# Reordering VectorE's work in the fused mLSTM and gated feed-forward kernel: weighing, decay differences and state additions in chunks 1 to 4

## The chip, the cores and the metric

The kernel runs on one core of a Trainium2 chip. The metric is the device time of one execution in microseconds (us); lower is better. The engines are called PE (TensorE's matrix products; PEld is its weight loads), DVE (VectorE), ACT (ScalarE), POOL (GpSimd) and SP (SyncE, which issues most DMAs). "L459" is line 459 of the kernel.

## The reference

Two blocks follow each other: an mLSTM cell over 4 batches, 8 heads, 768 steps and head width 40, and a feed-forward block on its output as 3072 tokens of width 320.

```python
for t in range(S):
    m_new = np.maximum(f_gate[:, :, t] + m, i_gate[:, :, t])
    f_stab = np.exp(f_gate[:, :, t] + m - m_new)
    i_stab = np.exp(i_gate[:, :, t] - m_new)
    m = m_new
    C = f_stab[..., None, None] * C + i_stab[..., None, None] * np.einsum('bhd,bhe->bhde', vt, kt)
    n = f_stab[..., None] * n + i_stab[..., None] * kt
    h_tilde = np.einsum('bhde,bhe->bhd', C, qt)
    nq = np.einsum('bhd,bhd->bh', n, qt)[:, :, None]
    y[:, :, t] = sigmoid(o_gate[:, :, t]) * h_tilde / np.maximum(np.abs(nq), 1.0)
x = y as (B * S, H * D)
h = x @ w_in            # 320 -> 2048
g = h * np.cos(h)
out = g @ w_out         # 2048 -> 320
```

## The kernel before

**Tiling.** The 768 steps are cut into 6 chunks of 128. A *cell* is one chunk of one batch with all 8 heads; cell n is chunk n // 4 of batch n % 4, so there are 24. Within a cell the recurrence is done in its chunkwise form: a 128 x 128 table of decays per head weighs the scores of queries and keys, and a state per batch (`st`, 40 x 41 per head) carries what earlier chunks left.

**The main loop.** `both_parts(c, b)` is a pair of *slots*. In each slot the feed-forward block does the up-projection of 256 hidden features for the 512 tokens of chunk c (class `Up`) and, later in the slot, a part of a down-projection (`down`, `down_first`, by a written plan). Beside that work, the pair computes one cell of the next chunk, n = 4 (c + 1) + b. So chunk c = 1 handles cells 8 to 11, chunk 2 cells 12 to 15, chunk 3 cells 16 to 19 and chunk 4 cells 20 to 23; chunk 5 has no cell. The first slot of a pair is called the even slot here, the second the odd slot. Chunk 0 has weights to prepare as well and an order of its own; from cell 7 on (`TURNED`) a cell works with its result transposed.

**Up.** An up-projection fills two PSUM tiles `pup`, halves e = 0 and 1, from a pool of two buffers: the next slot's `pup` of a half can only begin when this slot's gates have read it. Per half: ACT rounds (`near`, L639), DVE takes the remainder (`rest`, L642), ACT takes the sine (`sin`, L647, which gives a cosine of h by the quarter turn added before), and DVE multiplies (`gate`, L659, two instructions a half; L654 in chunk 0).

**The cell in the even slot.**
- `scores(n)` on PE writes two PSUM tiles `ps` (L453). They come from the pool `ps_a`, which has two buffers and also serves `hp` and `pu` below.
- `weigh(n)` on DVE multiplies them into the decays `E` (L459, two instructions).
- `decay_exponents(n + 1)` is the first step of the next cell's decays: a difference on DVE (L375, 128 x 1024), and a mask on POOL (L376). `decay(n + 1)` is the exponential on ACT (L384).
- `values_turned(n)` on PE writes two tiles `hp` from the state (L490) and from the weighed scores (L496).
- `normalize_turned(n)` on DVE (L510 to L522) reads `hp` and writes the next chunk's input, partly by a detour through DRAM; `fade(n)` multiplies the state by its decay (L577, two instructions, DVE).

In some even slots a down-projection ends and DVE also adds its parts together (`put_together`, seven L765) ahead of L510.

**The cell in the odd slot.** `seam(n)` on PE computes the state's increment `pu` (L596). `state(n)` on DVE adds it to `st` (L612, two instructions). `turn_blocks(n + 1)` and `turn_gates(n + 1)` (L414 to L425) prepare the next cell.

**POOL** does the mask, the sums `sg` of gated tiles for the down-projection (`sums`, L723), the weighing of keys (`kw`, L397), and in chunk 1 differences `T` of the output weights (L696).

**Order.** The whole program is under `tc.manual_schedule()`: each engine executes its instructions in the order in which this Python code emits them, and waits on semaphores for its inputs and for buffers that come free.

Of the kernel before, what the change touches and what calls it, by code (L numbers as in the profile page):

```python
# [29 lines left out]
def kernel(  # L30
# [39 lines left out]
    TURNED = 2 * B - 1  # L70
# [238 lines left out]
    def sigmoid(c, bs=slice(0, B)):  # L309
        o = sig[c][:, bs.start * DM:bs.stop * DM]  # L310
        nc.scalar.activation(out=o, in_=o, func=AF.Sigmoid)
# [53 lines left out]
    def psum_o():  # L365
        return ps_o.tile([128, HP, C], FP, name="pm", tag="o")

    def cols(n, j, width):
        c, b = divmod(n, B)
        return tab[:, c, j, ts(b, H)].unsqueeze(2).to_broadcast([128, H, width])  # L370


    def decay_exponents(n):
        E = Es[n]
        nc.vector.tensor_tensor(out=E, in0=E, in1=cols(n, 0, C), op=OP.subtract)  # L375
        nc.gpsimd.affine_select(out=E, in_=E, compare_op=OP.is_ge, fill=1.0e30, base=0,  # L376
                                pattern=[[0, H], [1, C]], channel_multiplier=-1)
# [5 lines left out]
    def decay(n):  # L383
        nc.scalar.activation(out=Es[n], in_=Es[n], func=AF.Exp, scale=-1.0)  # L384
# [61 lines left out]
    def scores(n):  # L446
        pool, tag = psum(n)
        qT, kT = qkT[n]
        ps = [pool.tile([128, HP, C], FP, name="ps", tag=tag) for _ in range(2)]
        for p in range(HP):  # L450
            for j in range(2):
                r = slice(64 * j, 64 * j + (64 if n < TURNED else D))
                nc.tensor.matmul(ps[j][:, p], kT[r, p], qT[r, p], start=True, stop=True)  # L453
        pss[n] = ps

    def weigh(n):
        for j in range(2):
            w = Es[n].rearrange("p (a j) t -> p a j t", j=2)[:, :, j]
            nc.vector.tensor_tensor(out=w, in0=pss[n][j], in1=w, op=OP.mult)  # L459

    def values_kept(n):

        pool, tag = (ps_o, "o") if n == B else psum(n)
        heads_of[n] = None
        if n >= B:
            pq = pool.tile([128, H, D1], FP, name="pq", tag=tag)
            for p in range(HP):
                nc.tensor.matmul(pq[:, 2 * p:2 * p + 2].rearrange("p j d -> p (j d)"), qkT[n][0][:, p],
                                 st[n % B][:, p].rearrange("p j d -> p (j d)"), start=True, stop=True)
            heads_of[n] = pq  # L470
# [94 lines left out]
    def halves(n):  # L565
        for j in range(2):
            r = slice(64 * j, 64 * j + D)
            yield j, r, st[n % B][r, :, j]
# [37 lines left out]
    def state(n):  # L606
        if n < N - B:
            for j, r, s in halves(n):
                if n < B:
                    nc.scalar.copy(out=s, in_=pus[n][r])  # L610
                else:
                    nc.vector.tensor_tensor(out=s, in0=s, in1=pus[n][r], op=OP.add)  # L612
# [101 lines left out]
    def sums(T):  # L714

        for c, s, p, in_parts in plan.get(T, ()):
            if in_parts:
                S = p2.tile([128, 4, C], FP, name="sg", tag="wt")
                A11, A21, A12, A22 = (gs[c, p, s][:, ts(i, C)] for i in range(4))
                engine = nc.vector if T > 8 * NC + 1 else nc.gpsimd  # L720
                for i, (x, y, op) in enumerate(((A21, A22, OP.add), (S[:, 0], A11, OP.subtract),
                                                (A11, A21, OP.subtract), (A12, S[:, 1], OP.subtract))):
                    engine.tensor_tensor(out=S[:, i], in0=x, in1=y, op=op)  # L723
                sg[c, s, p] = S
# [109 lines left out]
    def warm(k, bank=None):  # L834

        for _ in range(k):
            nc.tensor.matmul(bank or pw, nil, nil.unsqueeze(1).to_broadcast([128, HP, 128]), start=True, stop=True)
# [129 lines left out]
    def out_parts():  # L967
        p, piece = outs.pop(0)
        return p, parts(*piece)

    def out_join(p, h, last=None):
        join(*h, last)
        if p + 3 < NF // 2:
            outs.append((p + 3, weights_out(p + 3)))

    def both_parts(c, b):

        n = (c + 1) * B + b
        cell = n < N
        begin = c == b == 0
        more = cell and n + 1 < N
        f2 = 2 * b
        slot = NF // 2 * c + f2
        sums(slot)
        up = Up(c, f2, cell_after_first if begin else None)
        if cell:
            scores(n)  # L990
            if begin:
                values_kept(n)

                warm(6, psum_o())
        for e in range(2):
            up.near(e)
        if begin:
            weigh(n)
        for e in range(2):
            up.rest(e)  # L1000
        if cell and not begin:
            weigh(n)
        if begin or more and c > 0:
            decay_exponents(n + 1)
        for e in range(2):
            up.sin(e)
            up.gate(e)
        if n == TURNED:
            turn_gates(n)
        if c == 0 and b == 1:  # L1010
            sigmoid(1, slice(1, B))
        if begin:
            sigmoid(1, slice(0, 1))
        h = ()
        if c == 0 and not begin:
            out_join(*out_parts())
        if pieces:
            h = parts(*pieces.pop(0))
        rests = []
        ends = any(step[2] == NP - 1 for step in plan.get(slot, ()))  # L1020
        if ends:
            rests = down(slot)
        if begin or more and c > 0:
            decay(n + 1)
        elif more:
            decay_by_bias(n + 1)
        if 0 < slot <= NP:
            down_first(slot - 1)
        elif slot and not ends:
            down(slot)  # L1030
        for rest in rests:
            rest()
        if cell:
            if n < TURNED:
                load(n + 2)
                if not begin:
                    values_kept(n)
                values(n)
                normalize(n)
                if h:  # L1040
                    join(*h)
            else:
                values_turned(n)
                if h:
                    join(*h)

                normalize_turned(n)
                if n + 2 < N:
                    load(n + 2, "q")
                last_in(n)  # L1050
                if n + 2 < N:
                    load(n + 2, "bkv")
            if TURNED <= n + 2 < N:
                load_G(n + 2)
            if n + 3 < N:
                load_E(n + 3)
            if b == B - 2 and c + 2 < NC:
                load_o(c + 2)
            fade(n)
            if n + 1 == TURNED:  # L1060
                turn_blocks(n + 1)
        h = ()
        sin_next()
        if pieces:
            h = parts(*pieces.pop(0))
        sums(slot + 1)
        up = Up(c, f2 + 1)
        if cell:
            seam(n)
        for e in range(2):  # L1070
            up.near(e)
        for e in range(2):
            up.rest(e)
        if cell and n < TURNED:
            seam_out(n)
        if cell:
            state(n)
        if h:
            join(*h)
        for e in range(2):  # L1080
            up.sin(e)
            up.gate(e)
        if b == B - 1 and 0 < c < NC - 2:
            sigmoid(c + 2)
            sin_next()
        if more:
            weigh_k(n + 1)
        if c == 1 and b < B - 1:
            two_differences(2 * b + 2)
        if pieces:  # L1090
            join(*parts(*pieces.pop(0)))
        if c == 0:
            down_first(f2)
        else:
            for rest in down(slot + 1):
                rest()
        if pieces:
            join(*parts(*pieces.pop(0)))
        if c == 0:
            if b + 2 < B:  # L1100
                pieces.extend(weights_in(b + 2))
            h = out_parts()
        if more and n + 1 < TURNED:
            turn(n + 1)
            turn_out(n + 1, c > 0)
        elif more and n + 1 > TURNED:
            turn_blocks(n + 1)
        if c == 0:
            out_join(*h)
            if b == B - 1:  # L1110
                more_units()
                two_differences(0)
                sigmoid(2)
                sin_next()
        if more and n + 1 > TURNED:
            turn_gates(n + 1)
# [43 lines left out]
```

## Time and profile before

| | before |
|---|---|
| time, median of 3 runs | 533.53 us (532.84 to 539.57) |
| the profiled execution's own time | 533.63 us |
| span of its profile | 531.9 us |
| granted PE clock | 0.998 |
| PE busy | 519.4 us, 98% |
| PE weight loads | 343.2 us, 65% |
| DVE busy | 395.9 us, 74% |
| ACT busy | 264.7 us, 50% |
| POOL busy | 210.0 us, 39% |

The span runs from the first to the last instruction of the program; the execution's own time is 1.7 us longer. Busy times of engines overlap. Matrix products are pipelined and their ends are modelled, so a wait of PE can lie within its busy time. In lines of the timeline the first number is the start in us from the beginning of the span, the second the length; then engine, line, operation, written tile <- read tiles, shapes and the count of merged instructions. A bracket at the end gives idle time ahead of it and what ended it. PE does pairs of chunk 1 from 127.6 to 205.3, of chunk 2 to 281.9, of chunk 3 to 361.7 and of chunk 4 to 440.5.

### The profile page before, as it was taken

The numbers are of one execution on the slowest core, as the hardware profiler recorded it, in microseconds if no ns is written. First come the engines' busy times: TensorE is split into PE (matmuls) and PEld (weight loads), VectorE is DVE, ScalarE is ACT, GpSimd is POOL, SyncE is SP. The second block draws the span as 40 slices with busy tenths as digits, with TensorE's granted clock in tenths as the row PEclk, the third lists the DMA queues.
The fourth block names the chain that finished last, engine by engine and source line by source line (L and its number), as shares of the span: only waits on it lengthen the run. The fifth ranks groups of instructions, "written<-read, shape, count | busy, mean of one in ns | idle before, by whom it ended". The sixth has DMA issues, their size and how long they took to land.

```text
span 531.9 us, 10613 instructions
## 1 busy us (share of the span) xinstructions
PE 519.4 (98%) x3855; PEld 343.2 (65%) x3855; DVE 395.9 (74%) x864; ACT 264.7 (50%) x418; POOL 210.0 (39%) x409
## 2 busy tenths in 40 slices
PE   8989999999999999999999999999999999999996
PEld 6956565555565656556656577577577576657596
DVE  6797858889888987977978978978878864325253
ACT  4799696676633546453457354357354232313210
POOL 7523333434925631131522533533434425344350
PEclk9999999999999999999999999999999999999999
DMA  9999999813465376266276256356354100000000
GB/s 133 229 232 237 219 219 228 197 33 84 126 129 106 74 148 141 77 133 137 58 146 145 76 110 129 87 138 138 85 105 86 41 11 25 6 0 26 0 26 25
DMA packets 134860, 57.80 MB, mean 109 GB/s; under 512 B 70248, under 2 KB 130872, under 8 KB 134808
## 3 DMA queue, kind: packets, MB, share of 16 engines
q1 hardware_dynamic: 134664, 56.93, 48.5%
q8 instruction: 30, 0.49, 0.4%
q14 instruction: 22, 0.18, 0.1%
q0 software_dynamic: 96, 0.18, 0.1%
q10 hardware_dynamic: 48, 0.02, 0.0%
HBM read 50.76 MB, written 6.34 MB: 107 GB/s over the span
## 4 chain that ended last, share of the span: by engine, by line
PE 71%; DVE 13%; DMA 5%; issue 3%; SPq 3%; ACT 3%; POOL 1%; DVEq 0%; POOLq 0%; ACTq 0%
PE po L727 27%; PE pup L631 26%; PE pup L634 8%; PE po L823 3%; PE ps L453 2%; PE hp L496 2%; DVE n L642 2%; DVE E L375 2%; DMA o<-in_o_gate_dram 1%; DVE E L459 1%; SPq L332 1%; PE hp L490 1%; DMA bits<-in_moe_w_in_dram 1%; DMA ks<-in_k_dram 1%; DVE wt L148 1%
## 5 line engine op out<-in xcount | busy, mean ns | idle before, releaser
L631 PE MATMUL pup<-xT,w_in_sb 128*128 128x512 f32 x384 | 175.3, 599 | 4.5 <-DVE g L654 2.5
L639 ACT ACTIVATE n<-pup 128x512 int32<-128x512 f32 x96 | 52.0, 593 | 179.7 <-PE pup L634 179.7
L642 DVE SCALAR_TENSOR_TENSOR n<-pup,n 128x512 f32<-128x512 f32 x96 | 61.8, 686 | 92.8 <-ACT n L639 92.6
L631 PEld LDWEIGHTS pup<-xT,w_in_sb 128*128 128x128 f32 x384 | 69.6, 190 | 78.5 <-issue 64.5
L376 POOL TENSOR_SCALAR_AFFINE_SELECT E<-E 128x1024 f32<-128x1024 f32 x19 | 20.8, 1094 | 129.4 <-DVE E L375 123.5
L727 PE MATMUL po<-T,sg 128*128 128x160 f32 x426 | 69.5, 299 | 0.0
L647 ACT ACTIVATE n<-n 128x512 f32<-128x512 f32 x96 | 59.0, 631 | 16.3 <-DVE n L642 16.3
L727 PEld LDWEIGHTS po<-T,sg 128*128 128x128 f32 x426 | 61.7, 190 | 0.0
L723 POOL TENSOR_TENSOR sg<-g 128x128 f32<-128x128 f32 x66 | 30.2, 458 | 63.3 <-PE po L727 44.3
L634 PE MATMUL pup<-xT,w_in_l 64*128 64x512 f32 x192 | 54.2, 641 | 0.6 <-DVE w_in_l L149 0.6
L723 POOL TENSOR_TENSOR sg<-gg 128x128 f32<-128x128 f32 x66 | 30.2, 457 | 39.1 <-PE po L727 37.0
L634 PEld LDWEIGHTS pup<-xT,w_in_l 64*128 64x128 f32 x192 | 14.4, 184 | 37.0 <-issue 33.4
L727 PE MATMUL po<-w_out_sb,g 128*128 128x160 f32 (+1 forms) x180 | 38.3, 341 | 0.0
L823 PE MATMUL po<-w_out_sb,g 128*128 128x320 f32 x128 | 36.6, 439 | 0.7 <-POOL w_out_sb L149 0.7
L727 PEld LDWEIGHTS po<-w_out_sb,g 128*128 128x128 f32 x180 | 27.8, 189 | 11.0 <-issue 6.8
L414 DVE STREAM_TRANSPOSE t<-qs 128x512 f32<-128x512 f32 x34 | 34.9, 1108 | 0.0
L384 ACT ACTIVATE E<-E 128x1024 f32<-128x1024 f32 x21 | 22.2, 1058 | 25.2 <-POOL E L376 22.0
L727 PE MATMUL po<-w_out_sb,gg 128*128 128x160 f32 (+1 forms) x168 | 34.0, 329 | 0.0
L459 DVE TENSOR_TENSOR E<-ps,E 128x512 f32<-128x512 f32 x48 | 30.7, 681 | 2.5 <-ACT E L384 2.1
L659 DVE SCALAR_TENSOR_TENSOR g<-pup,n 128x256 f32<-128x256 f32 x82 | 30.7, 417 | 1.1 <-issue 0.6
L453 PEld LDWEIGHTS ps<-t,t 40*128 40x128 f32 (+1 forms) x384 | 25.0, 188 | 9.7 <-issue 9.2
L727 PE MATMUL po<-w_out_sb,sg 128*128 128x160 f32 x142 | 30.9, 299 | 0.0
(171 smaller groups left out, 847.3 us busy)
## 6 DMA issues: line engine op xcount, KB each, us to landing
E<-M_d SPq DMA_DIRECT2D x22, 512.0 KB
bits<-in_moe_w_in_dram SPq DMA_DIRECT2D x40, 128.0 KB
bits<-in_moe_w_out_dram SPq DMA_DIRECT2D x8, 640.0 KB
room<-G_d SPq DMA_DIRECT2D x34, 128.0 KB
ks<-in_k_dram SPq DMA_DIRECT2D x24, 160.0 KB
vs<-in_v_dram SPq DMA_DIRECT2D x24, 160.0 KB
out_dram<-o SPq DMA_DIRECT2D x18, 160.0 KB
o<-in_o_gate_dram SPq DMA_DIRECT2D x68, 40.0 KB
```

The source lines that it names most:

```text
L414: nc.vector.transpose(out=dst.rearrange("r p (t x) -> r p x t", x=T4), in_=src.rearrange("r p (x d) -> r p x d", x=T4)[:, :, :, 0:32])
L453: nc.tensor.matmul(ps[j][:, p], kT[r, p], qT[r, p], start=True, stop=True)
L459: nc.vector.tensor_tensor(out=w, in0=pss[n][j], in1=w, op=OP.mult)
L631: nc.tensor.matmul(pu, w_in_sb[:, i, ts(block(f2, e), 128)], x(i), start=(i == 0), stop=False)
L634: nc.tensor.matmul(pu, w_in_l[r, f2], x(NK, r), start=False, stop=True)
L639: nc.scalar.activation(out=self.n[e], in_=self.pu[e], func=AF.Copy, bias=0.25)
L642: nc.vector.scalar_tensor_tensor(out=self.n[e].bitcast(FP), in0=self.pu[e], scalar=0.25, in1=self.n[e], op0=OP.add, op1=OP.subtract)
L647: nc.scalar.activation(out=r, in_=r, func=AF.Sin, scale=TWO_PI_DOWN)
L659: nc.vector.scalar_tensor_tensor(out=gs[c, f2, s][:, ts(e, W)], in0=self.pu[e][:, ts(s, W)], scalar=TWO_PI, in1=n[:, ts(s, W)], op0=OP.mul ...
L723: engine.tensor_tensor(out=S[:, i], in0=x, in1=y, op=op)
L727: nc.tensor.matmul(out, g, w, start=start, stop=stop, skip_group_check=True)
L823: nc.tensor.matmul(po[0][b], gs[0, f // 2, f % 2][:, ts(b, C)], w_out_sb[:, f], start=(f == 0), stop=(f == NF - 1))
```

## The change

In the even slots of chunks 1 to 4, the two weighings go between the remainder of half 0 and the remainder of half 1, and the difference for the next cell goes behind the gates. In the odd slots, from cell 7 on, the additions to the state go behind the gates. Chunk 0 is otherwise as it was.

```diff
@@ both_parts, even slot
         if begin:
             weigh(n)
-        for e in range(2):
-            up.rest(e)
-        if cell and not begin:
+        up.rest(0)
+        if cell and c > 0:
             weigh(n)
-        if begin or more and c > 0:
+        up.rest(1)
+        if c == 0 and not begin:
+            weigh(n)
+        if begin:
             decay_exponents(n + 1)
         for e in range(2):
             up.sin(e)
             up.gate(e)
+        if more and c > 0:
+            decay_exponents(n + 1)
         if n == TURNED:
             turn_gates(n)
@@ both_parts, odd slot
         if cell and n < TURNED:
             seam_out(n)
-        if cell:
+        if cell and n < TURNED:
             state(n)
         if h:
             join(*h)
         for e in range(2):
             up.sin(e)
             up.gate(e)
+        if n >= TURNED and cell:
+            state(n)
```

Seen on the engines, the order of DVE changes so (cell 9's pair; the list is of instructions in program order):

```
even slot, before: L642 L642 L459 L459 L375 L659 L659 L659 L659 L510 ...
even slot, after:  L642 L459 L459 L642 L659 L659 L659 L659 L375 L510 ...
odd slot, before:  L642 L642 L612 L612 L659 L659 L659 L659 L414 ...
odd slot, after:   L642 L642 L659 L659 L659 L659 L612 L612 L414 ...
```

The orders of PE, ACT, POOL and SP are the same in both.

## The prediction

> **What bounds the kernel now.** I read the page's busy times, then busy time by stage, then single instructions of one stage, because the page's TensorE share says only that there is little to win.
>
> ```profile
> PE 519.4 (98%) x3855; PEld 343.2 (65%) x3855; DVE 395.9 (74%) x864; ACT 264.7 (50%) x418; POOL 210.0 (39%) x409
> ```
>
> TensorE (PE) is idle 12.5 us of 531.9. In the table by stage (window, its length, busy time of PE, PEld, DVE, ACT, POOL) each row is one pair of chunks 1 to 4, a pair being two slots and one cell; these are five of them:
>
> ```profile
> 167.30:186.30 19.00, 18.88 (x159) 11.62 (x158) 16.38 (x35) 8.46 (x12) 9.61 (x20) 1.00 0.48 101
> ...
> 264.00:281.90 17.90, 16.90 (x150) 10.03 (x148) 14.87 (x33) 9.17 (x13) 5.04 (x10) 1.00 0.65 135
> 281.90:301.30 19.40, 18.75 (x163) 12.09 (x163) 17.55 (x42) 11.95 (x17) 8.72 (x19) 1.00 0.49 113
> 301.30:321.50 20.20, 20.20 (x179) 13.84 (x178) 16.94 (x37) 8.46 (x12) 8.69 (x19) 1.00 0.51 108
> 321.50:341.60 20.10, 20.10 (x178) 13.74 (x177) 17.51 (x42) 8.74 (x13) 8.70 (x20) 1.00 0.50 111
> ```
>
> From 301.3 on PE never pauses: nothing that VectorE (DVE) does earlier can be gained there, and chunk 4 lies wholly in that part. Before it, some pairs lose a little. The timeline of the pair of cell 15 (start, length, instruction) shows where:
>
> ```profile
> 269.39 1.29 DVE L642 SCALAR_TENSOR_TENSOR n<-pup,n 128x512 f32<-128x512 f32 x2 [1.93 <-ACT n L639]
> ...
> 270.60 1.28 DVE L459 TENSOR_TENSOR E<-ps,E 128x512 f32<-128x512 f32 x2
> ...
> 271.59 1.00 PE L490 MATMUL hp<-room,st 40*32 40x128 f32 x32
> 271.79 1.22 DVE L375 TENSOR_TENSOR E<-E,tab 128x1024 f32<-128x1024 f32 x1
> 271.93 0.40 PEld L490 LDWEIGHTS hp<-room,st 40*32 40x32 f32 x30 [0.20 <-DVE E L459]
> ...
> 272.53 1.08 PE L496 MATMUL hp<-E,vs 128*32 128x128 f32 x32
> 272.93 1.41 DVE L659 SCALAR_TENSOR_TENSOR gg<-pup,n 128x256 f32<-128x256 f32 x4
> ...
> 273.73 0.30 PEld L631 LDWEIGHTS pup<-xT,w_in_sb 128*128 128x128 f32 x2 [0.39 <-DVE gg L659]
> 273.73 3.70 PE L631 MATMUL pup<-xT,w_in_sb 128*128 128x512 f32 x8
> ```
>
> PE waits twice in the even slot. `hp` takes the PSUM banks of `ps`, so its second half waits for the second weighing: L490 takes 1.00 here and 0.67 in pairs with a longer `po` ahead (234.63, 330.96), a loss of 0.33. The next `pup` waits for the first gates: 1.20 after the start of L496 against 1.01 at 236.23 and 332.57, a loss of 0.19. "PE busy" hides most of this: the L490 wait is inside its 1.00.
>
> Scanned this way, the losses of chunks 1 to 4 are: 0.47 to 0.53 in the even slots of cells 9, 10, 11, 12, 14, 15 and 16 (all with only 14 `po` matmuls); 0.9 at the end of cell 15's odd slot, where `po` is short too (PE waits for L659 until 281.92); 0.17 and 0.5 before `pu` of cells 12 and 16 (219.80 and 296.94: PE waits for L519); 0.07 at 301.29. That is 5.2 us in all, 1% of the span: the ceiling of any gain.
>
> **What the Trainium skill says.** "Perfetto Trace Analysis", section "Identifying the Most-Contended Engine", holds that matmul busy share is no measure of headroom for TensorE. The trace agrees: the waits above lie inside busy time, so I count gaps by hand. "VectorE: DVE Perf Modes", section "The DRAIN you can't avoid", says that a wait between two Vector operations adds nothing to their spacing. Here two L642 of 0.69 last 1.29 together, so the second starts 0.60 after the first; I use such steps and charge no fee for a new order. "ScalarE: Activation LUTs", section "What ACT_TABLE_LOAD costs", gives about 1283 ns for a table load and about 1380 ns of drain; the trace has 1283 ns, and the next operation 0.01 to 0.02 us behind it, so I take 1.28 alone. "SBUF — State Buffer", section "SBUF: two separate sides", says that Vector operations with two SBUF inputs and GpSimd operations exclude each other on a shared port. The trace fits: the two L577 last 0.67 with POOL idle (277.70) and 1.21 beside POOL's `T` differences (162.28).
>
> **The change, part by part.** Nothing is added or removed: 32 weighings (L459, cells 8 to 23), 15 differences (L375) and 26 state additions (L612, cells 7 to 19) move on DVE. PE, ACT and SP keep their order; POOL keeps its order and waits for its mask (L376) as before, but the mask now follows a later L375. No DMA and no queue entry moves.
>
> Even slot, counted from the start t of the first L642 (269.39 in the sample). Before: remainders 0 and 0.60; weighings 1.20 and 1.80; difference 2.40; gates 3.54, 3.87, 4.20, 4.53; what follows, 4.86. After: remainder 0; weighings 0.60 and 1.20 (their scores end at 269.57, before t+0.60); second remainder 1.80, done 2.49; gates of half 0 at 2.40 and 2.73, since sin of half 0 ended long ago; second sin 2.54 to 3.17; gates of half 1 at 3.21 and 3.54; difference 3.87 to 5.09; what follows, 5.01.
>
> - Weighing ends at t+1.88 instead of 2.48. PE asks for it at t+2.20. The L490 wait goes.
> - The first gates end at t+3.15 instead of 4.29, the last at 3.96 instead of 4.95. PE, now 0.33 earlier, asks at about t+3.81 and t+4.26. The `pup` wait goes.
> - DVE idles about 0.15 for the second sin, so normalizing starts at 5.01 instead of 4.86.
> - The difference ends 1.47 later. Mask 0.13 behind it, 1.09 long; exp 1.06; table load 1.28; the `spot` step 0.20: ScalarE (ACT) is free for the odd slot's L639 at t+8.94. In the sample that is 278.33, whereas `pup` is ready at 278.05 (it was 278.58). So 0.28 of slack is overspent, but from L639 to the end of half 0's gates takes 2.8 (0.61 + 0.02 + 0.69 + 0.05 + 0.63 + 0.04 + 0.33 + 0.42), and PE has 0.44 of `pu` and 4.0 or more of `po` to do meanwhile: 1.6 left. Cost nothing, except in cell 15.
> - POOL's sums and `kw` behind the mask come 1.5 later. `kw` is for the next cell; first use of `sg` in the sample is 279.50, its sums then end near 277.6. Nothing.
>
> Odd slot: the two L612 took 0.70 of DVE ahead of the gates (280.41 to 281.11) and now take it behind. The new `st` is read four cells on; `pu`'s bank is wanted by the next scores about 4 us later. Where PE had no wait there, gain nothing.
>
> The sum over cells:
> - 9, 10, 11, 14: the even wait goes, 0.47 + 3 x 0.53 = 2.06.
> - 15: the odd slot. Remainder at about 279.15 (POOL now runs beside L521 to L577, which slows them), half 0's gates end near 281.30, PE goes on at 281.35 instead of 281.92: 0.57 for the pair.
> - 12 and 16: the seven L765 additions stand ahead of L510 to L519, and `pu` waits for L519. PE arrives 0.5 earlier and waits 0.5 longer; the 0.15 is lost: 2 x -0.15.
> - 7, 8, 13, 17 to 23: no wait now, none made: 0.
>
> Total 2.06 + 0.57 - 0.30 = 2.3 us. The profiled execution took 533.63 (span 531.9), within 0.1 of the median 533.53: 533.6 - 2.3 = 531.3.
>
> What the trace doesn't show is how much DVE's two-SBUF-input operations slow down where POOL's sums shift onto them: 0 at best, and at worst the full difference of L513, L521, L522 and L577 (0.2 + 0.2 + 0.3 + 0.54, about 1.2) in a pair. I take 0.2 in cell 15 and nothing elsewhere, since in 9 and 10 POOL runs beside them already.
>
> **Rivals.**
> - Nothing moves. PE's earlier arrival is spent at the next wait everywhere, as I expect for cells 12 and 16: `pu` or the odd slot's gates, held by ACT's late exp. For: ACT loses its slack of 1.74 in short pairs. Against: 1.6 of cover behind it. Time: 533.6.
> - All waits go. The odd slot of cell 15 and the `pu` waits vanish too: 533.6 - 5.2 = 528.4. Against: L519 stands behind the same DVE work as before.
> - Slower. The mask and the sums on POOL, 1.5 later, fall on normalizing and fading (L512 to L577), and the odd slot's remainders come about 1 us late. This decides where DVE has no idle time between L577 and L642: cells 12, 15, 16 and 18 (at 338.07 and 338.10 they touch), once the lateness passes the 0.3 to 0.7 left ahead of the next `pup`. Four pairs at about 1 us each, and about 1.5 of the gain left: 533.6 + 4.0 - 1.5 = 536.1. Against: L765 delays normalizing in 12, 16 and 18 until POOL is mostly done.
>
> **How the numbers follow.** Forecast 0.64, nothing moves 0.15, all waits go 0.07, slower 0.14. Two per cent, about what a measurement of this kernel can tell from no change, is 10.7 us: twice the ceiling of the gain, so faster gets 0.01; slower by so much needs 0.7 in every pair, beyond my worst case, and gets 0.06 for what I overlook; within 2%, 0.93. The range runs from 529.3 (nearly all waits gone) to 535.2 (most of the slower case).
>
> **What would show it.** Right: L490 at 0.67 in cells 9 to 16; `pup` 1.01 after L496; L375 behind the gates with the mask about 1.5 later; `pu` of cells 12 and 16 waiting about 1.2 instead of 0.5 in the worse one; windows from 301.3 on as long as before. Wrong: a new PE wait in an odd slot released by L659, L642 or ACT; L577 at 1.2 where it had 0.67, followed by late remainders; or a chain of waits that goes through L375, mask and exp into L639.

## The result, and the profile after

The changed kernel takes 532.29 us in the median of 20 runs; 20 runs of the kernel before, taken for this comparison, have a median of 535.63 (the three earlier ones, from which the forecast starts, had 533.53). The ratio is 0.9939, 95% interval 0.9918 to 0.9961; a second comparison of the same two kernels (e11) gave 0.9966, 0.9944 to 0.9988. The forecast, 531.3 of 533.6, is a ratio of 0.9957 and lies in both. Some executions of each kernel that was run often had a mean granted clock of 0.987 instead of 0.994 to 1.000, and took longer: in the second comparison 539.46 to 539.60 before (7 of 43) and 537.55 to 537.63 with the change (3 of 22), 1.9 less; 536.48 to 536.60 in e10 below (3 of 22).

The page of the profiled execution (span 530.9), busy times:

```profile
PE 518.6 (98%) x3855; PEld 343.8 (65%) x3855; DVE 404.5 (76%) x864; ACT 264.7 (50%) x418; POOL 210.0 (40%) x409
```

DVE is busy 8.6 us longer with the same 864 instructions. That is the first thing to notice: at its new places some of the work goes slower, or overlaps less with its neighbour on DVE. The table by stage, windows cut at the starts of the pairs of cells 10, 15, 16, 17 and 18:

```profile
167.80:186.30 18.50, 18.50 (x159) 11.47 (x157) 17.32 (x35) 8.35 (x12) 9.56 (x20) 1.00 0.47 103
...
263.10:280.80 17.70, 16.54 (x151) 9.94 (x149) 16.40 (x35) 8.67 (x13) 5.22 (x10) 1.00 0.61 131
280.80:300.20 19.40, 18.82 (x162) 12.39 (x162) 18.08 (x42) 12.43 (x17) 8.67 (x19) 1.00 0.50 122
300.20:320.50 20.30, 20.30 (x179) 13.91 (x178) 17.67 (x39) 8.49 (x12) 9.13 (x19) 1.00 0.52 109
320.50:340.60 20.10, 20.10 (x178) 13.75 (x178) 17.51 (x40) 8.75 (x13) 8.67 (x20) 1.00 0.46 105
```

PE has no gap left in pair 10; from 300 on the pairs are as long as before. The timeline of cell 15's pair, whose first L642 starts at 268.50:

```profile
268.50 0.69 DVE L642 SCALAR_TENSOR_TENSOR n<-pup,n 128x512 f32<-128x512 f32 x1 [0.80 <-ACT n L639]
...
269.11 1.28 DVE L459 TENSOR_TENSOR E<-ps,E 128x512 f32<-128x512 f32 x2
...
270.31 0.68 DVE L642 SCALAR_TENSOR_TENSOR n<-pup,n 128x512 f32<-128x512 f32 x1
...
270.70 0.67 PE L490 MATMUL hp<-room,st 40*32 40x128 f32 x32
270.90 1.54 DVE L659 SCALAR_TENSOR_TENSOR gg<-pup,n 128x256 f32<-128x256 f32 x4
...
271.30 1.08 PE L496 MATMUL hp<-E,vs 128*32 128x128 f32 x32
...
272.31 3.70 PE L631 MATMUL pup<-xT,w_in_sb 128*128 128x512 f32 x8
272.36 1.22 DVE L375 TENSOR_TENSOR E<-E,tab 128x1024 f32<-128x1024 f32 x1
273.49 0.51 DVE L510 STREAM_TRANSPOSE room<-hp 128x128 f32<-128x128 f32 x2
273.71 1.09 POOL L376 TENSOR_SCALAR_AFFINE_SELECT E<-E 128x1024 f32<-128x1024 f32 x1 [8.54 <-DVE E L375]
274.03 0.79 DVE L512 SCALAR_TENSOR_TENSOR room<-room,least 128x8 f32<-128x8 f32 x1
```

L490 takes 0.67 instead of 1.00, and L631 starts 1.01 after L496 instead of 1.20: both waits of the even slot are gone. The odd slot of cell 15 still ends in a wait, and `pu` waits in cells 12 and 16 (waits of PE, in total, times, longest, from 149 to 380):

```profile
PE pu L596 <- DVE room L519: 1.3, 2, 0.7
PE pup L631 <- DVE g L659: 1.2, 1, 1.2
```

The prediction expected about 1.2 for the longer wait of `pu`. Here the two are 0.68 (cell 12) and 0.58 (cell 16); in e11, the same code, 0.15 and 1.05. The difference lies ahead of them: cell 16's even slot is 0.5 longer here than in e11 (9.77 against 9.29), as PE waits there for the transfer `xT<-X_d`, and in e11 it is cell 12's that is longer, by 0.6 (9.76 against 9.19). The pairs as a whole have the same length in both.

**A steadier measure.** The time from one even slot's first L631 to the next repeats within about 0.1 us (most pairs within 0.02) between profiles of the same code, while the opening does not: cell 9's even slot started at 148.34 before and at 149.32 after, and 0.97 of this 0.98 is there already at the even slot of cell 7 (105.98 and 106.95), up to which the two do the same. (In e3 below cell 9 began only at 154.21, so its whole time of 539.49 says nothing on its edit.) So the profiled spans differ by only 1.0, but the *stretch* from cell 9's to cell 20's even slot fell from 213.39 to 211.39, by 2.00. By pairs:

| pair of cell | 9 | 10 | 11 | 12 | 13 | 14 | 15 | 16 | 17 | 18 | 19 | stretch |
|---|---|---|---|---|---|---|---|---|---|---|---|---|
| before | 18.94 | 19.00 | 19.00 | 19.36 | 20.63 | 18.75 | 17.90 | 19.37 | 20.20 | 20.12 | 20.12 | 213.39 |
| changed | 18.47 | 18.47 | 18.54 | 19.48 | 20.63 | 18.22 | 17.64 | 19.47 | 20.22 | 20.12 | 20.13 | 211.39 |
| e1, even part only | 18.82 | 19.03 | 18.58 | 19.49 | 20.62 | 18.50 | 18.20 | 19.92 | 20.22 | 20.12 | 20.12 | 213.62 |
| e2, state only | 18.94 | 18.99 | 19.00 | 19.36 | 20.62 | 18.75 | 17.46 | 19.37 | 20.12 | 20.12 | 20.12 | 212.85 |
| e3, weighing only | 18.94 | 19.00 | 19.00 | 19.35 | 20.62 | 18.75 | 17.91 | 19.36 | 20.20 | 20.12 | 20.12 | 213.37 |
| e4, difference only | 18.75 | 18.86 | 18.89 | 19.36 | 20.62 | 18.56 | 17.97 | 19.80 | 20.22 | 20.12 | 20.12 | 213.27 |
| e5, ScalarE delayed | 18.57 | 18.48 | 18.48 | 19.48 | 20.63 | 18.22 | 18.18 | 19.47 | 20.23 | 20.12 | 20.12 | 211.98 |
| e7, as e1, no mask | 18.47 | 18.47 | 18.47 | 19.70 | 20.63 | 18.22 | 17.38 | 19.18 | 20.19 | 20.12 | 20.12 | 210.95 |
| e8, parts later | 18.48 | 18.47 | 18.54 | 19.28 | 20.73 | 18.22 | 17.65 | 19.92 | 20.23 | 20.12 | 20.12 | 211.76 |
| e9, parts and fade later | 18.48 | 18.47 | 18.47 | 19.08 | 20.63 | 18.22 | 17.05 | 19.63 | 20.21 | 20.12 | 20.12 | 210.48 |
| e10, e9 and earlier loads | 18.47 | 18.48 | 18.47 | 19.08 | 20.63 | 18.22 | 17.05 | 19.51 | 20.23 | 20.12 | 20.12 | 210.38 |
| e11, changed again | 18.47 | 18.47 | 18.55 | 19.52 | 20.62 | 18.22 | 17.65 | 19.45 | 20.23 | 20.12 | 20.13 | 211.43 |

(Cells of the table are differences of starts in the PE timeline; a sum can differ from the last column by 0.02.)

### The profile page after: what moved, and what is told of

It is laid out like the page before. It is cut to its first block, busy times and chain, and to the rows that moved or that the text cites. A ratio compares the mean times of both kernels' runs of the same rounds, so it can differ in the third digit from the quotient of the medians.

```text
span 530.9 us, 10605 instructions
## 1 busy us (share of the span) xinstructions
PE 518.6 (98%) x3855; PEld 343.8 (65%) x3855; DVE 404.5 (76%) x864; ACT 264.7 (50%) x418; POOL 210.0 (40%) x409
## 4 chain that ended last, share of the span: by engine, by line
PE 73%; DVE 8%; SPq 6%; ACT 6%; DMA 4%; issue 2%; POOL 0%; DVEq 0%; ACTq 0%; POOLq 0%
PE po L727 29%; PE pup L631 26%; PE pup L634 8%; SPq L332 4%; PE hp L496 3%; PE po L823 3%; PE ps L453 2%; DMA bits<-in_moe_w_in_dram 2%; PE hp L490 2%; DVE n L642 1%; SPq L129 1%; DMA qs<-in_q_dram 1%; PE pu L596 1%; ACT n L639 1%; ACT wt L138 1%
## 5 line engine op out<-in xcount | busy, mean ns | idle before, releaser
L631 PE MATMUL pup<-xT,w_in_sb 128*128 128x512 f32 x384 | 175.4, 599 | 3.2 <-DVE g L654 1.8
L639 ACT ACTIVATE n<-pup 128x512 int32<-128x512 f32 x96 | 51.8, 590 | 149.0 <-PE pup L634 149.0
L642 DVE SCALAR_TENSOR_TENSOR n<-pup,n 128x512 f32<-128x512 f32 x96 | 63.2, 685 | 80.0 <-ACT n L639 79.7
L631 PEld LDWEIGHTS pup<-xT,w_in_sb 128*128 128x128 f32 x384 | 69.6, 190 | 76.8 <-issue 65.5
L727 PE MATMUL po<-T,sg 128*128 128x160 f32 x426 | 69.4, 299 | 0.0
L727 PEld LDWEIGHTS po<-T,sg 128*128 128x128 f32 x426 | 61.7, 190 | 0.0
L634 PE MATMUL pup<-xT,w_in_l 64*128 64x512 f32 x192 | 54.7, 641 | 0.6 <-DVE w_in_l L149 0.6
L634 PEld LDWEIGHTS pup<-xT,w_in_l 64*128 64x128 f32 x192 | 14.7, 184 | 37.2 <-issue 33.4
L727 PE MATMUL po<-w_out_sb,g 128*128 128x160 f32 (+1 forms) x180 | 38.3, 341 | 0.0
L727 PEld LDWEIGHTS po<-w_out_sb,g 128*128 128x128 f32 x180 | 27.8, 189 | 11.0 <-issue 6.8
L727 PE MATMUL po<-w_out_sb,gg 128*128 128x160 f32 (+1 forms) x168 | 34.0, 329 | 0.0
L659 DVE SCALAR_TENSOR_TENSOR g<-pup,n 128x256 f32<-128x256 f32 x82 | 31.1, 417 | 2.1 <-ACT n L647 0.8
L659 DVE SCALAR_TENSOR_TENSOR gg<-pup,n 128x256 f32<-128x256 f32 x78 | 29.8, 418 | 2.1 <-ACT n L647 1.2
```

The source lines that it names most:

```text
L631: nc.tensor.matmul(pu, w_in_sb[:, i, ts(block(f2, e), 128)], x(i), start=(i == 0), stop=False)
L634: nc.tensor.matmul(pu, w_in_l[r, f2], x(NK, r), start=False, stop=True)
L639: nc.scalar.activation(out=self.n[e], in_=self.pu[e], func=AF.Copy, bias=0.25)
L642: nc.vector.scalar_tensor_tensor(out=self.n[e].bitcast(FP), in0=self.pu[e], scalar=0.25, in1=self.n[e], op0=OP.add, op1=OP.subtract)
L659: nc.vector.scalar_tensor_tensor(out=gs[c, f2, s][:, ts(e, W)], in0=self.pu[e][:, ts(s, W)], scalar=TWO_PI, in1=n[:, ts(s, W)], op0=OP.mul ...
L727: nc.tensor.matmul(out, g, w, start=start, stop=stop, skip_group_check=True)
```

## The experiments

### e1: the even-slot part alone

```diff
-        if cell and n < TURNED:
+        if cell:
             state(n)
...
-        if n >= TURNED and cell:
-            state(n)
```

> Only the even-slot part of the change: weighing between the remainders, the difference behind the gates; the additions to the state stay ahead of the gates. Measure: the stretch from the even slot's first L631 of cell 9 to that of cell 20, 213.39 us before and 211.39 with the whole change. My theory: the waits in the even slots of cells 9, 10, 11 and 14 go as with the whole change (2.0), but the odd slots of cells 15 and 16, where VectorE is late, lose the 0.4 to 0.5 each that the state behind the gates gave: about 212.2. Rival, that the move of the state does nothing: 211.4.

Measured: 213.62, a little longer than before. Both the theory and the rival were too kind: all of the gain is gone, and not only in cells 15 and 16. Cell 10's pair shows how, in the timeline of this kernel's odd slot:

```profile
185.44 1.29 DVE L642 SCALAR_TENSOR_TENSOR n<-pup,n 128x512 f32<-128x512 f32 x2
...
186.65 0.65 DVE L612 TENSOR_TENSOR st<-st,pu 40x164 f32<-40x164 f32 x2
...
187.31 1.42 DVE L659 SCALAR_TENSOR_TENSOR g<-pup,n 128x256 f32<-128x256 f32 x4
...
188.12 1.12 PE L631 MATMUL pup<-xT,w_in_sb 128*128 128x512 f32 x2 [0.30 <-DVE g L659]
```

The gates now come behind the state and PE waits for them; the bracket names only the part of the wait outside PE's modelled busy time. Counted from the first L642 of the pair (at 174.57 here, at 173.17 in the changed kernel), L642 of this slot comes at 10.87 here and 10.86 there, the first gate at 12.74 and 12.25, and L631 at 13.55 and 13.09, there without a wait. Against the changed kernel the pairs of 9, 10, 14, 15 and 16 are 0.35, 0.56, 0.28, 0.56 and 0.45 longer.

### e2: the state alone

```diff
-        if cell:
+        if cell and n < TURNED:
             state(n)
...
+        if n >= TURNED and cell:
+            state(n)
```

> Only the odd-slot part: the additions to the state behind the gates. My theory: it acts where TensorE waited for gates in an odd slot, that is in the pair of cell 15 (wait 0.9 to about 0.35) and by 0.07 in that of cell 16, and nowhere else: stretch 213.39 - 0.6 = 212.8. Rival, that earlier gates help every odd slot a little: 13 cells, each pair shorter, below 212.3.

Measured: 212.85, 0.54 below before, 0.44 of it in cell 15 and 0.08 in 17 (whose start holds the wait at cell 16's end). This is what the theory had, within 0.1. So e1 and e2 alone sum to -0.31 (+0.23 and -0.54), together they bring -2.00.

### e3 and e4: weighing alone, the difference alone

```diff
 # e3: weigh between the remainders, the difference ahead of the gates
+        up.rest(0)
+        if cell and c > 0:
+            weigh(n)
+        up.rest(1)
...
         if begin or more and c > 0:
             decay_exponents(n + 1)
 # e4: both remainders, then weigh; the difference behind the gates
-        if begin or more and c > 0:
+        if begin:
             decay_exponents(n + 1)
...
+        if more and c > 0:
+            decay_exponents(n + 1)
```

> Only the weighing goes between the remainders; the difference stays ahead of the gates, the state too. My theory: the wait inside L490 (0.33) goes, but the gates come at the same time as before, so that the wait ahead of the next L631 grows by as much, from 0.19 to about 0.52: stretch 213.4, as before. Rival, that each edit removes its own wait: L490 at 0.67 and pairs 9, 10, 11 and 14 shorter by 0.3 each, stretch 212.1.

> Only the difference goes behind the gates; weighing stays behind both remainders, the state ahead of the gates. My theory: the wait inside L490 stays (1.00), the one ahead of L631 goes (1.01 after L496): 0.2 in each of the pairs of cells 9, 10, 11 and 14, nothing in 12, 15 and 16; stretch 213.39 - 0.8 = 212.6. Rival, that the difference ahead of the gates was the whole cost: 0.5 in each, 211.4 to 211.6.

Measured: e3 213.37, as before in every pair. Weighing now ends early and L490 takes 0.67, but the gates come no earlier: L631 starts 1.54 after L496 instead of 1.21. In cell 10 of e3:

```profile
180.73 0.67 PE L490 MATMUL hp<-room,st 40*32 40x128 f32 x32
181.33 1.08 PE L496 MATMUL hp<-E,vs 128*32 128x128 f32 x32
182.87 3.70 PE L631 MATMUL pup<-xT,w_in_sb 128*128 128x512 f32 x8 [0.46 <-DVE gg L659]
```

e4 213.27: cells 9, 10, 11 and 14 gain 0.19, 0.14, 0.11 and 0.19, about as expected, but 16 loses 0.43 and 15 0.07, so 0.12 is left of the 0.8. In cell 16 the odd slot's L642 comes 0.45 later, with L521 ahead of it at 0.92 instead of 0.43; e7 below takes this up. The waits of PE from 149 to 365 in e4 name the gates as well as `pu`:

```profile
PE pup L631 <- DVE g L659: 1.5, 2, 1.2
PE pu L596 <- DVE room L519: 0.9, 2, 0.7
```

### e5: ScalarE later on purpose

```diff
         h = ()
+        if more and c > 0:
+            for _ in range(6):
+                nc.scalar.copy(out=spot, in_=spot)
         sin_next()
```

> The changed kernel with six more one-element copies on ScalarE (0.2 us each) between the exponential and the next table load of every even slot of chunks 1 to 4, so that L639 of the odd slot can start 1.2 us later. Stretch from the even slot of cell 9 to that of cell 20: 211.39 without. My theory: in the changed kernel the odd slot is paced by VectorE's L577, which ends 1.5 after L639 has delivered in cell 10 and 0.6 after it in cell 15; so only cell 15 loses, about 0.7: 212.1. Rival, that the late exponential on ScalarE paces the odd slots: 1.2 in each of the pairs of cells 9, 10, 11, 14 and 15, 217.

Measured: 211.98; cell 15 loses 0.54, cell 9 0.10, the pairs of 10, 11 and 14 nothing. In cell 10 L639 starts 1.2 later (9.94 after the first L642 of the pair, 8.74 without the copies), and the odd slot's L642 at 10.86 in both. So the late exponential does not pace cell 10's odd slot in the changed kernel; VectorE does. In cell 15 the margin was smaller than the 1.2.

### e7: the even part without the mask

```diff
         if more and c > 0:
-            decay_exponents(n + 1)
+            decay_exponents(n + 1, False)    # L375 stays, the mask L376 is left out
```

> The kernel with the even-slot part alone (stretch 213.62; pair of cell 10 19.03, of cell 15 18.20), and POOL's mask L376 left out for cells 9 to 23, so the decays above the diagonal are not cut off and the output is not the reference's. My theory: the mask, now beside L512 instead of beside the gates, and the sums and kw behind it, now beside L521, slow these operations by 0.3 and 0.5, and L642 of the odd slot comes that much later; without the mask L512 falls from 0.72 to about 0.4 and everything on POOL comes 1.1 earlier: pairs of cells 9, 10, 14 and 15 shorter by 0.3 to 0.6, stretch about 212. Rival, that only the order on VectorE makes the odd gates late: stretch unchanged, 213.5.

Measured: 210.95, shorter by 2.67 than e1, more than expected, and with the state still ahead of the gates. Pairs 9, 10 and 14 are as short as in the changed kernel, 15 and 16 shorter by 0.82 and 0.74 than in e1. Only cell 12 got longer, by 0.21. The expectation had POOL's work come 1.1 earlier, but in the pairs of cells 10 and 15 the first sum behind the mask starts 2.5 earlier: without the mask POOL does not wait for the late L375 either. In cell 14 four sums that stood behind the mask are even done before it would have begun. What VectorE did in cell 10's pair in three kernels: first before the change, then the changed kernel, then e7 (one line further down, L513 is L512, L522 is L521):

```profile
178.06 0.41 DVE L512 SCALAR_TENSOR_TENSOR room<-room,least 128x8 f32<-128x8 f32 x1
...
180.27 0.44 DVE L521 TENSOR_TENSOR room<-room,room 128x256 f32<-128x256 f32 x1
```

```profile
178.31 1.09 POOL L376 TENSOR_SCALAR_AFFINE_SELECT E<-E 128x1024 f32<-128x1024 f32 x1 [8.42 <-DVE E L375]
178.70 0.72 DVE L512 SCALAR_TENSOR_TENSOR room<-room,least 128x8 f32<-128x8 f32 x1
...
181.19 0.72 POOL L397 TENSOR_TENSOR kw<-ks,tab 128x320 f32<-128x320 f32 x1
181.27 0.91 DVE L521 TENSOR_TENSOR room<-room,room 128x256 f32<-128x256 f32 x1
```

```profile
178.37 0.29 DVE L513 SCALAR_TENSOR_TENSOR room<-room,least 128x8 f32<-128x8 f32 x1
...
180.47 0.63 DVE L522 TENSOR_TENSOR room<-room,room 128x256 f32<-128x256 f32 x1
```

In the changed kernel L512 ends with the mask (178.70 + 0.72 = 179.42, the mask 179.40), and L521, started beside `kw`, ends 0.27 behind it (182.18 and 181.91). Before, the mask lay beside the gates, and L512 beside the sums. e7 also lets the exponential come earlier, but that is not what helped cell 10: in e1 its odd L642 starts 0.02 behind the last L577 (185.44 and 185.42), while L639 was done by 184.37. So POOL's late work, the mask and what stands behind it, is what made the odd gates late. e7 moves both together; the durations tell them apart. From the first L642 to the odd slot's, cell 10 takes 0.97 longer in the changed kernel than before: about 0.12 from the second sine, 0.31 at L512 beside the mask, and 0.47 at L521 beside `kw`.

### e8, e9 and e10: following the waits that are left

```diff
 # e8, in normalize_turned, behind the two L519; L765 and the stores come here
+        for step in between:
+            step()
 # e9, besides: the fade from ahead of the odd slot to behind its gates
-            fade(n)
+            if n <= TURNED:
+                fade(n)
...
         if n >= TURNED and cell:
+            if n > TURNED:
+                fade(n)
             state(n)
 # e10, besides
-            if b == B - 2 and c + 2 < NC:
+            if b == (B - 2 if c == 0 else B - 3) and c + 2 < NC:
                 load_o(c + 2)
```

> The changed kernel with the seven additions L765 (and the stores behind them) moved behind the two L519 instead of ahead of L510 in the even slots where a down-projection ends. My theory: the waits of pu for L519 in the pairs of cells 12 and 16 (0.68 and 0.58) vanish, nothing else moves: pairs 19.48 and 19.47 become 18.8 and 18.9, stretch 211.39 - 1.3 = 210.1. Rival, that VectorE's total is the bound there: then the wait goes to the gates of the odd slot, and the pairs keep their length, 211.4.

> The kernel with the additions L765 behind L519, and besides the fading of the state (two L577, 0.67 to 1.23 us) moved from ahead of the odd slot's remainders to behind its gates, just before the state's additions. My theory: the odd slot's L642 then starts when ScalarE has delivered, 0.6 earlier in cell 15: its pair falls from 17.64 to about 17.1, the others stay: stretch 209.5. Rival, that cell 15 is bound by ScalarE's exponential and table load: 210.1, as without this step.

> The kernel with the additions L765 behind L519 and the fading behind the gates, in which TensorE waited 0.8 at the end of cell 16's first up-projection for the transfer xT<-X_d; SP had been issuing the 16 loads of the output gates ahead of it. Here these loads are issued one pair earlier in chunks 1 to 3. My theory: SP's queue held the transfer, the wait of 0.8 goes, pair of cell 16 from 19.63 to about 18.9, stretch 210.48 - 0.8 = 209.7; in total about 1.5 below the changed kernel and 4 below the kernel before, ratio 0.992 to 0.993 plus what the opening does. Rival, that the transfer comes late because VectorE writes the tile late: stretch 210.5.

Measured: e8 211.76; the waits of `pu` for L519 vanish from the list of waits, but cell 16 is 0.45 longer and cell 12 only 0.20 shorter. The rival was right that the wait goes to the gates (PE waits 2.6 for them from 148 to 362, 1.2 without this step); that the stretch grows by 0.37 neither had foreseen. e9 210.48: cell 15 drops to 17.05, as expected, but 16 then waits for a transfer, and 1.0 of the forecast is missing. The timeline and the list of waits (278 to 300) of e9, where L636 is L634, L633 is L631 and L661 is L659:

```profile
283.92 1.12 PE L636 MATMUL pup<-xT,w_in_l 64*128 64x512 f32 x3 [0.81 <-DMA xT<-X_d]
```

```profile
PE pup L636 <- DMA xT<-X_d: 0.8, 1, 0.8
PE pup L633 <- DVE g L661: 0.6, 1, 0.6
```

e10 does remove that wait, as the waits from 148 to 362 show, and it comes back at the gates (L729 is L727, L778 is L765):

```profile
PE pup L633 <- DVE g L661: 1.4, 2, 0.8
PE po L729 <- DVE hs L778: 0.3, 1, 0.3
```

The stretch is 210.38, so 0.1 of the 0.8 is won: with the loads elsewhere the transfer comes in time, but VectorE is the next limit in cell 16. e10 is the shortest stretch with the whole computation, 3.0 below before and 1.0 below the changed kernel. Its measured ratio to before is 0.9947 (0.9924 to 0.9969), beside 0.9966 (0.9944 to 0.9988) for the changed kernel in the same comparison. The intervals overlap; that e10 is faster than the changed kernel rests on the stretches. The longest executions, given with the result, agree with them: 2.9 to 3.0 us below those before, 1.0 below those of the changed kernel.

### e11: the changed kernel again

> The changed kernel once more, on the same chip and beside the same runs of the kernel before: the pairs of cells 9 to 19 take as long as in its first profile within 0.1 each (stretch 211.4), while the start of cell 9's even slot, which was 149.3 here and 127.5 to 133.3 for cell 8's in other profiles, moves by some us with the same code. If the ratio of 0.9939 comes from the stretch alone (2.0 of 533) it should lie near 0.996; if the opening differs in fact, near 0.994.

Measured: stretch 211.43, every pair within 0.04; cell 9 began at 150.36. The ratio 0.9966 is a gain of about 1.8 us, what the stretch gives; 0.9939 would be 3.3. A gain of 2.0 of 533.6 is a ratio of 0.9963: inside this interval, and 0.0002 above the first one. No pair explains what the first comparison had beyond 2.0. A part is the mixture of executions: 6 of its 20 runs before took 538.98 to 539.57, of the 20 changed ones one took 537.60, and without these the means differ by 2.6 instead of 3.6. The rest stays open.

## Why the prediction was right

- *The bound.* Right. PE was full from 300 on, and the gain lay only in pairs where PE had waited: 9, 10, 11, 14 and 15.
- *The even slot's times.* Right within 0.02 up to L510: second remainder 1.81 after t (1.80), gates 2.40 (2.40), difference 3.86 (3.87), L510 4.99 (5.01), the mask 5.21 (5.22). ScalarE started L639 at 8.81 (8.94).
- *The two waits of the even slot.* Right: both went (0.67 and 1.01). The runs add that they hang together: weighing alone gives nothing (e3), the difference alone 0.1 to 0.2 in four pairs (e4).
- *Cells 12 and 16.* Right in length: +0.12 and +0.10 for the forecast +0.15 each. Where PE waits instead varies between profiles: at `pu`, or at the transfer ahead of it.
- *Cells 9, 10, 11, 14.* 2.06 forecast, 0.47 + 0.53 + 0.46 + 0.53 = 1.99 measured.
- *Cell 15.* Forecast -0.57, measured -0.26. The term that was mis-sized is "I take 0.2 in cell 15 and nothing elsewhere" for POOL's work beside VectorE. L642 of the odd slot started 10.01 after t, not 9.76. From L512 to the next operation took 0.36 longer than before, beside the mask, and from L521 to the next 0.50 longer, beside `kw` (L512 0.79 and L521 0.91, each 0.43 before). The prediction's list of what POOL can slow left out L512 and gave L521 0.2.
- *"Nothing elsewhere", and "gain nothing" in the odd slots.* Both wrong, and they cancelled: that was luck. In cell 10 L642 came 10.86 after the first one (184.03 - 173.17), against 9.89 before and 10.04 by the prediction's terms (0.15 later). Its reason, that in 9 and 10 POOL runs beside these operations already, did not hold for L521: it had taken 0.44 there. Of the "1.6 left" for PE hardly 0.1 remained: half 0's gates end at about 186.17 (185.42 + 0.33 + 0.42) and PE asked at 186.26. It was enough because the state's 0.65 had gone behind the gates. Without that the change is worth nothing (e1). Outside cell 15 the state's move was priced at nothing; given the even part it is worth 213.62 - 211.39 = 2.2.
- *The slower rival.* Its mechanism was real: counted from the pair's first L642, the odd slot's came 0.95 and 0.97 later in cells 9 and 10, 0.57 in 16 and 18 and 0.40 in 14. The list of cells where DVE has no idle time ahead of this L642 was in part wrong: in the trace before they are 9, 10, 12, 14, 16 and 18, and in 15 DVE waits 0.84 for L639. What kept the lateness off the end was the third part of the same change. That ScalarE's late exponential paces the odd slots was refuted (e5): 1.2 more cost 0.54 in cell 15, 0.10 in cell 9 and nothing in 10, 11 and 14.

The total, 2.3 forecast and 2.0 in the stretch, was thus better than its parts: the even slots were understood, the odd slots came out by the cancelling.

## What to carry to other kernels

Price the parts of a reordering together: here the two halves alone came to 0.2 lost and 0.5 won, and to 2.0 won together, since the even part made the odd gates late and the state's move made up for it. When an instruction moves, look not only at who waits for it but at what will run *beside* it and beside its followers on other engines, and read the durations there again. For effects of a few tenths of a per cent, compare lengths of repeated stages between two profiles rather than whole times: they repeated within 0.1 us where the opening moved by 2 and, once, by 6. Whole times gave the same 2.0 and 3.0 within 0.1 once like executions were compared with like.

## What the runs showed of the hardware

- Beside a POOL mask of 1.09 a 128 x 8 VectorE operation (L512) took 0.72 to 0.79 (cells 9, 10, 11, 14 and 15 of the changed kernel) that took 0.29 in e7, beside a sum, and 0.17 with POOL idle (218.25 before). It ended within 0.02 of the mask. The Trainium skill ("SBUF — State Buffer", "SBUF: two separate sides") describes such an exclusion, for VectorE operations with two SBUF inputs; the runs show it for a tiny operation as well. The gates, which take one input from PSUM, were not slowed beside the mask: in the pair of cell 15 before, four L659 took 1.41 beside it, and 1.42 in the odd slot with POOL idle for most of them.
- DVE's busy time grew by 8.6 us with no instruction added, in a kernel that got faster: the longer L512 (0.72 for 0.41) and L521 (0.91 for 0.44) of cell 10, for example, count as busy throughout.
